# A forward table held twice and the work of the first steps laid out anew in a fused FFT filter and feed-forward kernel

## The chip, the cores and the metric

The kernel runs on one core of a Trainium2 chip. The metric is the device time of one execution in microseconds. TensorE (PE) multiplies matrices and writes PSUM, VectorE (DVE) and ScalarE (ACT) read PSUM and SBUF, GpSimd (POOL) and SyncE (SP) here only issue DMA transfers, each in its own queue, in order. POOL's transfers convert fp32 to fp16 on the way where the tiles differ in type; it has up to eight in flight, since it waits for the ninth last transfer's semaphore to be used again.

## The reference

`x` is [8, 3008, 256]: eight batches of 3008 tokens with 256 channels. Each channel is filtered in the frequency domain along the tokens, and the result goes through a feed-forward layer with a slope for negative values.

```python
X = np.fft.rfft(x, axis=1)
Y = X * (filt_r + 1j * filt_i)[None]
y = np.fft.irfft(Y, n=3008, axis=1).reshape(24064, 256)
h = y @ w_in                                       # 256 -> 2048
g = np.maximum(h, 0) + alpha * np.minimum(h, 0)
out = g @ w_out                                    # 2048 -> 256
```

## The kernel before, in words

**The transform.** 3008 is 94 x 32. A batch goes through four stages, each a set of small matmuls and evictions. Piece a (`piece_a`, eight per batch, L155) is the transform of length 94; ACT evicts it into `asb`, `save_a` stores `asb` to DRAM and `turn_a` reads it back as `at` in another layout. Piece b (`piece_b`, six per batch, L179) is the transform of length 32 with its twiddles from the table `twf_s`, and DVE multiplies the result by the filter and by a copy of the filter with rows exchanged (`filt_s`, `filts_s`, L186 and L187). The two products are added across partitions by transfers in POOL's queue: added into `uu` by the transfer itself for batch one (L191), and for later batches brought into `sw` (L193) and added by DVE (`piece_s`). Piece c (`piece_c`, six per batch, L210) is the inverse of length 32 with `twi_s`; ACT evicts it to `v`, and `turn_c` stores it to DRAM and, after the last piece, reads it back as `zt`. Pairs d (`pair_d`, eight per batch, L232) are the inverse of length 94 and evict to `yT`, the transposed input of the feed-forward layer. Group g of four (752 tokens each) of a batch is its pairs 2g and 2g+1.

**Batch zero** is done by a class of its own, `First`, without DRAM: it turns tiles by matmuls with a unit matrix (`turn_at` L289, `half_t` and `piece_t` L340), uses a second table `twx_s` so that no exchange of rows is needed, and goes in twelve passes `kp` (L408 to L419): `piece_b(kp + 2)` (L299), `piece_c(kp)` (L323), evictions to `v`. In its piece b every matmul uses a tile of 64 rows and 32 columns of PE, sixteen per pass, since each half of the table's 64 columns has to be written to two places of PSUM. DVE's multiplication per pass is L303. Its first pass takes the filter from an fp32 tile `fst`, loaded by SP; the others from `filt_s`, loaded by POOL as three parts (`load_filt`, rows 1 to 3, 4 to 7, 8 to 11). `fst` has the tag "asb": it shares its one buffer with batch one's `asb`. After the loop POOL copies `fst` into `filt_s` (L420) and builds `filts_s` from it (L423, L425); DVE later negates parts of `filts_s` (`neg`, L545). `warm` (L382) multiplies a unit matrix into a bank that is then overwritten: filling work for PE. `half_t` and `half_d` of group zero end this part.

**The feed-forward layer** runs in 48 blocks of 512 or 384 tokens, twelve for two batches, 16 steps each: 768 steps. In step j a block's `up` does two matmuls of 512 columns (L466); after every second one ACT evicts both (L475) into a ring of nine slots `gtb`, and DVE does the slope with `alm_s` (L478, two per eviction; L480 once per four steps). `down` (L497, four matmuls per step for 512 tokens) is that of the block before. ACT evicts the output to `osb` (L502) and SP stores it (L448).

**The order** is written out by hand (`manual_schedule`): engines execute in program order, and semaphores follow from the tiles. A dictionary `plan` says which pieces go into which step (L506 to L562). They run before the step's `up`; in a step that has a piece a or c (`front`) the step's `down` goes first. The first block has no block before it, so steps 0 to 15 have no `down`. Before the change batch zero's groups one to three lie in steps 0 to 33 (L536 to L542): group one as halves, groups two and three as whole pieces. Batch one has its pieces a at even steps 12 to 26, `turn_a` at 28, pieces b at 36 to 66 (every six steps), pieces c at 48 to 78, pairs d from 91. The loads of x for batch two are put at steps 17 to 29; they are POOL instructions and wait in its queue, not for the step itself but for a free buffer (four of them, `p_x`) and for the instructions ahead. `banks(False)` is one PSUM tile `psF` of two banks with one buffer; `banks(True)` is `hps`, two buffers, which `up`, pieces a and c share; `bank("o")` is `op`, two buffers.

**Tables and slopes.** SP loads the tables of batch zero in two parts, columns 0 to 8 first (L364, L367) and 8 to 24 after the sixth piece a (L390 to L395). A tiny `memset` by DVE on the part to be loaded (L391) holds that load back until then. The slopes come from `al16` by a transpose on PE (L397) and two DVE instructions (L398, L399) after the sixth piece a.

Of the kernel before, what the change touches and what calls it, by code (L numbers as in the profile page):

```python
# [16 lines left out]
D = 256  # L17
# [33 lines left out]
def kernel(  # L51
# [211 lines left out]
    class First(Fft):  # L263
        def __init__(self):
            super().__init__(0)
            self.at = p_fft.tile([128, NK, D], FP16, name="at")
            self.v = p_fft.tile([128, NK, D], FP16, name="v")
            self.zt = p_fft.tile([96, N2, D], FP16, name="zt")
            self.fst = p_fft.tile([128, 1, 2, D], FP32, name="fst", tag="asb")
            self.am = gtb[:, 0:6].rearrange("p a b c -> p (a b c)")  # L270
            self.vm = self.v.rearrange("p k d -> p (k d)")

# [19 lines left out]
        def piece_b(self, kp):  # L292
            hp = psH.tile([128, 2, 512], FP32, name="hps").rearrange("p r (i d) -> p r i d", i=2)
            for i in range(2):
                for par in range(2):
                    r = slice(64 * par, 64 * par + 64)
                    for o in (0, 32, 64, 96):
                        k = 2 * kp + o // 64
                        nc.tensor.matmul(hp[o : o + 32, par, i], twf_s[r, k, 32 * i : 32 * i + 32],  # L299
                                         self.at[r, k], start=True, stop=True, tile_position=(64 * par, o))  # L300
            uu = p_uw.tile([128, 2, 2, D], FP16, name="uu", bufs=3)
            fl = self.fst if kp < 1 else filt_s
            nc.vector.tensor_mul(uu, hp, fl[:, kp].unsqueeze(2).to_broadcast([128, 2, 2, D]))  # L303
            self.uw[kp] = uu

        def piece_c(self, kp):
            if kp % 2 == 0:
                self.ops = [psO.tile([128, 2, D], FP32, name="op") for _ in range(2)]
            if kp == 11:
                pf = banks(False)  # L310
                warm(5, pf[:, 0])
                self.ops = [pf[:, e].rearrange("p (k d) -> p k d", k=2) for e in range(2)]
            kb = 0 if kp == 11 else kp % 2
            u = self.uw.pop(kp)
# [1 line left out]
            for par in range(2):  # L316
                for f in range(2):
                    for i, t in enumerate((tw, tx)):
                        for e in range(2):
                            r = slice(64 * e, 64 * e + 64)  # L320
                            o = self.ops[e][:, kb].rearrange("p (g w) -> p g w", g=16)
                            o = o[:, 8 * f : 8 * f + 8, 8 * par : 8 * par + 8]
                            nc.tensor.matmul(o.rearrange("p g (c e) -> p g c e", c=2),  # L323
                                             u[r, par, i, 128 * f : 128 * f + 128], t[r, 2 * kp + par],
                                             start=(i == 0), stop=(i == 1))

        def keep_c(self, kp, evicts, n=2):
            vm = self.vm.rearrange("p (g q k e) -> p g q k e", q=4, k=NK, e=4)
# [31 lines left out]

    xc = {(0, c): load_x(0, c) for c in range(4)}
    f0 = First()
    load_filt(nc.sync, f0.fst, 0, 1)
    tables(nc.sync, ("twf",), 0, 8)  # L364
    nc.sync.dma_start(out=al16, in_=moe_alpha.rearrange("(j p) -> j p", p=128))
    nc.sync.dma_start(out=id32, in_=id32_d.ap())
    tables(nc.sync, ("twi", "twx"), 0, 8)  # L367
    load_filt(nc.gpsimd, filt_s, 1, 4)
    load_filt(nc.gpsimd, filt_s, 4, 8)
    load_filt(nc.gpsimd, filt_s, 8, 12)  # L370
# [15 lines left out]
    for i in range(8):  # L386
        f0.piece_a(i, both[i % 2], i % 3 < 2)
        if i % 2 == 1:
            warm((4, 4, 8, 3)[i // 2], bank("o"))
        if i == 5:  # L390
            nc.vector.memset(twf_s[:, 8:24, 0:1], 0.0)  # L391
            tables(nc.sync, ("twf", "twi", "twx"), 8, 24)
            nc.sync.dma_start(out=wi3_s, in_=consts["wi3"].ap())
            nc.sync.dma_start(out=wf1_s, in_=consts["wf1"].ap())
            nc.sync.dma_start(out=sgn_s, in_=sgn_d.ap())  # L395
            alp = psO.tile([128, 2, D], FP32, name="op")
            nc.tensor.transpose(alp[:, 0, 0:16], al16, id32)  # L397
            nc.vector.tensor_copy(al_s, alp[:, 0, 0:16])  # L398
            nc.vector.tensor_scalar(alm_s, al_s, 1.0, -1.0, OP.mult, OP.add)  # L399
    f0.turn_at(0, 1, on_act)  # L400
    f0.turn_at(1, 1, on_dve, True)
    warm(2, bank("o"))
# [25 lines left out]
        f0.half_t(i, evict, kind)  # L428
    for i, evict, kind, fill in ((0, on_act, "h", 1), (2, on_dve, "o", 0), (1, on_act, "o", 1), (3, on_dve, "f", 0)):
        f0.half_d(i, evict, kind, fill)  # L430


    sizes = [512] * 5 + [384] + [512] * 6
# [99 lines left out]
        for i in range(8):  # L533
            put(d_at[i], f.pair_d, i, on_act)

    for i in range(4):  # L536
        put(i, f0.half_t, 4 + i, both[i % 2], "o")
        put(6 + i, f0.half_d, 4 + (0, 2, 1, 3)[i], both[i % 2], "o")
    for g, ts, ds, evict in ((2, (13, 15), (21, 23), on_dve), (3, (25, 27), (31, 33), on_act)):
        for i in range(2):  # L540
            put(ts[i], f0.piece_t, 2 * g + i, evict)
            put(ds[i], f0.pair_d, 2 * g + i, evict)  # L542

    def neg(ha, hb):
        nc.vector.tensor_scalar(filts_s[:, ha:hb], filts_s[:, ha:hb], sgn_s[:, 0:1], None, OP.mult)  # L545

    for i in range(4):
        put(16 + 2 * i, neg, 3 * i, 3 * i + 3)

    def d_steps(p):  # L550
        return [p + t for t in (91, 93, 104, 108, 116, 120, 140, 152)]

    plan_fft(1, range(12, 28, 2), 28, 4, (17, 21, 25, 29), range(36, 72, 6), 0, range(48, 84, 6),
             (91, 93, 98, 101, 110, 120, 142, 154))
    plan_fft(2, (50, 56, 62, 68, 74, 80, 82, 84), 90, 4, (57, 69, 81, 85), (104, 114, 126, 136, 148, 158), 7,
             (114, 126, 136, 148, 158, 170), d_steps(96))
    for b in range(3, NB):
        p = 96 * (b - 1)
        a_at = (10, 16, 22, 28, 34, 36, 44, 48) if b == 3 else (6, 10, 18, 22, 30, 34, 42, 46)
# [53 lines left out]
```

## Time and profile before

| | |
|---|---|
| time, median of three | 786.81 us (785.9 to 788.47) |
| profiled execution: time | 788.27 us |
| profiled execution: span in the trace | 786.5 us |
| PE busy | 770.0 us (98%), 6450 matmuls |
| DVE busy | 596.2 us (76%) |
| ACT busy | 583.0 us (74%) |
| POOL busy (issuing transfers) | 142.3 us (18%) |
| first up-projection (L466) | 41.28 us |
| first eviction of batch one's piece a | 50.58 us |
| up-projection of step 16 | 56.37 us |
| up-projection of step 36 | 81.60 us |

The span runs from the first to the last record; the time has some 1.8 us around it. All places are microseconds from the span's start. A busy PE is not PE at its peak, because overlapping matmuls are all counted as busy; so stages are compared by the length of their steps, which the L466 records give, and by what PE waits for between them. "Idle before, releaser" in a timeline is the time that an engine stood still ahead of a group and what ended it; "issue" means that the profile shows nothing that it waited for. "DMA issues to landing" is measured from the start of the issuing instruction.

### The profile page before, as it was taken

To read this page: it belongs to the slowest core of one execution; us is meant where nothing else is said; L and a number is where in the kernel's file an instruction comes from. 1 tells how busy PE (TensorE), PEld (TensorE's weight loads), DVE (VectorE), ACT (ScalarE), POOL (GpSimd) and SP (SyncE) were. 2 spreads that over 40 slices of the span, in tenths; PEclk is the share of its full clock that TensorE was granted. 3 is DMA by queue.
4 is the path that set the end of the run, shared out by engine and by line. 5 is a ranking of instruction groups with operands and counts; after the bars stand their busy time and mean duration, and the time that the engine had idled before them with its cause. 6 is when DMAs were issued, how large, how long until landed. Compare 5 with 4: busy or idle time off the path is not lost.

```text
span 786.5 us, 16280 instructions
## 1 busy us (share of the span) xinstructions
PE 770.0 (98%) x6450; PEld 512.1 (65%) x6450; DVE 596.2 (76%) x1117; ACT 583.0 (74%) x671; POOL 142.3 (18%) x271
## 2 busy tenths in 40 slices
PE   7889999999999999999999999999999999999997
PEld 3556566666666666766666666766666666766665
DVE  3686895788868887788867888688877888766663
ACT  3578688788778887798777887788876777677663
POOL 6512362132202220022201222010100111000000
PEclk9999999999999999999999999999999999999999
DMA  9978688756664657555593655834474233511112
GB/s 197 166 162 194 148 162 171 229 132 158 140 167 109 145 137 146 136 119 130 126 200 88 143 125 134 191 82 108 115 148 129 56 86 93 143 42 28 41 41 55
DMA packets 95084, 100.66 MB, mean 128 GB/s; under 512 B 11280, under 2 KB 82464, under 8 KB 94816
## 3 DMA queue, kind: packets, MB, share of 16 engines
q1 hardware_dynamic: 80368, 70.25, 34.2%
q0 software_dynamic: 14640, 29.38, 21.6%
q8 instruction: 50, 0.82, 0.4%
q14 instruction: 26, 0.21, 0.1%
HBM read 55.28 MB, written 46.66 MB: 130 GB/s over the span
## 4 chain that ended last, share of the span: by engine, by line
PE 88%; DMA 8%; POOL 1%; ACT 1%; DVE 1%; issue 1%; SPq 0%; ACTq 0%; POOLq 0%
PE op L497 40%; PE hps L466 40%; DMA xs<-in_x_dram 3%; PE hps L155 3%; PE psF L232 2%; DMA a_dram<-asb 2%; PE psF L179 2%; PE hps L210 1%; DMA filts_s<-filt_s 1%; DMA filt_s<-fst 1%; DMA filt_s<-in_filt_r_dram 1%; POOL filt_s L122 1%; DMA at<-a_dram 1%; POOL xs L112 0%; ACT gtb L475 0%
## 5 line engine op out<-in xcount | busy, mean ns | idle before, releaser
L475 ACT ACTIVATE gtb<-hps 128x1024 f16<-128x1024 f32 (+1 forms) x384 | 385.8, 1005 | 136.9 <-PE hps L466 132.7
L466 PE MATMUL hps<-yT,win_s 128*128 128x512 f16 (+1 forms) x1536 | 435.1, 375 | 1.8 <-ACT gtb L475 1.5
L497 PE MATMUL op<-wout_s,gtb 128*128 128x256 f16 x3008 | 435.8, 273 | 0.1
L497 PEld LDWEIGHTS <-gtb 128*128 128x128 f16 x3008 | 294.0, 98 | 168.3 <-issue 0.4
L478 DVE TENSOR_SCALAR m<-gtb,alm_s 128x512 f16<-128x512 f16 (+1 forms) x768 | 232.9, 346 | 148.0 <-ACT gtb L475 147.1
L480 DVE TENSOR_TENSOR gtb<-gtb,m 128x2048 f16<-128x2048 f16 (+1 forms) x192 | 231.0, 1203 | 10.1
L466 PEld LDWEIGHTS <-win_s 128*128 128x128 f16 x1536 | 142.6, 98 | 59.7 <-issue 15.3
L193 POOL DMA_DIRECT2D sw<-ww x144 | 70.8, 500 | 383.8 <-DVE ww L186 380.9
L255 ACT ACTIVATE asb<-hps 96x1024 f16<-96x1024 f32 x56 | 57.1, 1020 | 11.7 <-PE hps L155 11.2
L502 ACT ACTIVATE osb<-op 128x512 f32<-128x512 f32 (+1 forms) x97 | 56.2, 579 | 5.3 <-issue 2.8
L255 ACT ACTIVATE v<-hps 128x1024 f16<-128x1024 f32 x42 | 43.0, 1024 | 14.3 <-PE hps L210 14.3
L255 ACT ACTIVATE yT<-psF 128x752 f16<-128x752 f32 x58 | 46.2, 797 | 8.5 <-PE psF L232 8.5
L112 POOL DMA_DIRECT2D xs<-in_x_dram x64 | 35.5, 597 | 92.0 <-PE hps L155 77.0
L186 DVE TENSOR_TENSOR ww<-psF,filts_s 128x1024 f16<-128x1024 f32 x42 | 51.1, 1216 | 0.0
L187 DVE TENSOR_TENSOR uu<-psF,filt_s 128x1024 f16<-128x1024 f32 x42 | 51.0, 1213 | 0.0
L155 PE MATMUL hps<-xs,wf_s 94*96 94x512 f16 x112 | 33.4, 379 | 0.2 <-ACT gtb L475 0.2
L232 PEld LDWEIGHTS <-zt 96*128 96x128 f16 x512 | 28.8, 98 | 5.0 <-issue 2.1
L232 PE MATMUL psF<-wi_s,zt 96*128 96x94 f16 x484 | 30.3, 206 | 0.5 <-DVE yT L258 0.5
L198 DVE TENSOR_TENSOR uu<-uu,sw 128x1024 f16<-128x1024 f16 x36 | 24.6, 684 | 1.2 <-DMA sw<-ww 1.2
L191 POOL DMA_DIRECT2D uu<-ww x24 | 19.2, 1219 | 28.0 <-DVE uu L187 23.7
L179 PE MATMUL psF<-at,twf_s 64*64 64x256 f16 x336 | 17.9, 281 | 1.8 <-DMA at<-a_dram 1.8
L210 PE MATMUL hps<-uu,twi_s 64*64 64x256 f16 x336 | 16.5, 271 | 0.0
(64 smaller groups left out, 175.0 us busy)
## 6 DMA issues: line engine op xcount, KB each, us to landing
out_dram<-osb SPq DMA_DIRECT2D x160, 128.0 KB
a_dram<-asb SPq DMA_DIRECT2D x28, 384.0 KB
v_dram<-v SPq DMA_DIRECT2D x84, 128.0 KB
zt<-v_dram SPq DMA_DIRECT2D x28, 384.0 KB
sw<-ww POOLq DMA_DIRECT2D x144, 64.0 KB, 2.5
at<-a_dram SPq DMA_DIRECT2D x20, 384.0 KB
xs<-in_x_dram POOLq DMA_DIRECT2D x32, 192.0 KB, 4.4
xs<-in_x_dram POOLq DMA_DIRECT2D x32, 184.0 KB, 5.8
```

Of the source, the lines that this page charges most:

```text
L155: nc.tensor.matmul(ps[0:96, u], wf1_s, xs[:, o : o + 512], start=True, stop=True)
L186: nc.vector.tensor_mul(ww, px, fs)
L187: nc.vector.tensor_mul(uu, px, f)
L193: nc.gpsimd.dma_start(out=sw[o : o + 32], in_=ww[i : i + 32])
L232: nc.tensor.matmul(ps[:, m], self.zt[:, 8 * g + 4 * mh + m, dh * 128 : dh * 128 + 128], wi3_s, start=True, stop=True)
L255: nc.scalar.activation(o, i, AF.Copy)
L466: nc.tensor.matmul(self.hps[:, j % 2, 0:tn], win_s[:, kt, j * 128 : (j + 1) * 128], yT[:, kt, self.t0 : self.t0 + tn], start=(kt == 0), st ...
L475: nc.scalar.activation(g[:, 2 * i : 2 * i + 2], self.hps[:, :, 0:tn], AF.Copy)
L478: nc.vector.tensor_scalar(m[:, 2 * i + h], g[:, 2 * i + h], 0.0, a, OP.min, OP.mult)
L480: nc.vector.tensor_add(g, g, m)
L497: nc.tensor.matmul(self.op[:, si - s0], self.gts[k][:, 128 * si : 128 * si + 128], wout_s[:, k], start=(si == s0 and k == 0), stop=(si == ...
L502: nc.scalar.activation(osb[:, 0:m], self.op[:, 0:m], AF.Copy)
```

## The change

In `First`, the forward table is kept a second time as `twd`, in a part of the ring `gtb` that is not in use yet, with each half of 32 columns written twice side by side, so that piece b needs eight matmuls with tiles of 64 rows and 64 columns instead of sixteen. `twice` makes it in three copies: columns 0 to 8 on ACT after the sixth piece a, 8 to 16 on ACT and 16 to 24 on DVE after the eighth. SP's loads are put in another order: table `twf` first, then `fst`, held back by a `memset` until the second piece a is evicted, and after the sixth piece a `twf`, `twi`, `twx`, the slopes and the small tables. The transpose of the slopes moves behind group zero. The last pass fills with two matmuls instead of five. Groups one to three are whole pieces, later than before for group two, and `neg` moves to steps 26 to 35. For batch one the pieces b and c move by two steps and some pairs d by one; the loads of x for batch two are put at 34, 42, 54 and 66 (between the pieces b), and some pieces of batch two move by two to four steps. Later batches keep their plan.

```diff
+            self.twd = gtb[:, 6:9].rearrange("p a b c -> p (a b c)").rearrange("p (k m) -> p k m", m=128)
...
-                    for o in (0, 32, 64, 96):
-                        k = 2 * kp + o // 64
-                        nc.tensor.matmul(hp[o : o + 32, par, i], twf_s[r, k, 32 * i : 32 * i + 32],
-                                         self.at[r, k], start=True, stop=True, tile_position=(64 * par, o))
+                    for e in range(2):
+                        nc.tensor.matmul(hp[64 * e : 64 * e + 64, par, i],
+                                         self.twd[r, 2 * kp + e, 64 * i : 64 * i + 64], self.at[r, 2 * kp + e],
+                                         start=True, stop=True)
...
-                warm(5, pf[:, 0])
+                warm(2, pf[:, 0])
...
+        def twice(self, ka, kb, copy):
+            o = self.twd[:, ka:kb].rearrange("p k (i c m) -> p (k i) c m", i=2, c=2)
+            w = twf_s[:, ka:kb].rearrange("p k (i m) -> p (k i) m", i=2)
+            copy(o, w.unsqueeze(2).to_broadcast([128, 2 * (kb - ka), 2, 32]))
...
-    load_filt(nc.sync, f0.fst, 0, 1)
     tables(nc.sync, ("twf",), 0, 8)
-    nc.sync.dma_start(out=al16, in_=moe_alpha.rearrange("(j p) -> j p", p=128))
-    nc.sync.dma_start(out=id32, in_=id32_d.ap())
-    tables(nc.sync, ("twi", "twx"), 0, 8)
...
+        if i == 1:
+            nc.vector.memset(f0.fst[:, 0, :, 0:1], 0.0)
+            load_filt(nc.sync, f0.fst, 0, 1)
         if i == 5:
+            f0.twice(0, 8, on_act)
             nc.vector.memset(twf_s[:, 8:24, 0:1], 0.0)
-            tables(nc.sync, ("twf", "twi", "twx"), 8, 24)
+            tables(nc.sync, ("twf",), 8, 24)
+            tables(nc.sync, ("twi", "twx"), 0, 8)
+            tables(nc.sync, ("twi", "twx"), 8, 24)
             nc.sync.dma_start(out=wi3_s, in_=consts["wi3"].ap())
+            nc.sync.dma_start(out=al16, in_=moe_alpha.rearrange("(j p) -> j p", p=128))
+            nc.sync.dma_start(out=id32, in_=id32_d.ap())
...
-            alp = psO.tile([128, 2, D], FP32, name="op")
-            nc.tensor.transpose(alp[:, 0, 0:16], al16, id32)
-            nc.vector.tensor_copy(al_s, alp[:, 0, 0:16])
-            nc.vector.tensor_scalar(alm_s, al_s, 1.0, -1.0, OP.mult, OP.add)
+    f0.twice(8, 16, on_act)
+    f0.twice(16, 24, on_dve)
     f0.turn_at(0, 1, on_act)
...
         f0.half_d(i, evict, kind, fill)
+    alp = bank("o")
+    nc.tensor.transpose(alp[:, 0:16], al16, id32)
+    nc.vector.tensor_copy(al_s, alp[:, 0:16])
+    nc.vector.tensor_scalar(alm_s, al_s, 1.0, -1.0, OP.mult, OP.add)
...
-    for i in range(4):
-        put(i, f0.half_t, 4 + i, both[i % 2], "o")
-        put(6 + i, f0.half_d, 4 + (0, 2, 1, 3)[i], both[i % 2], "o")
-    for g, ts, ds, evict in ((2, (13, 15), (21, 23), on_dve), (3, (25, 27), (31, 33), on_act)):
+    for g, ts, ds, te, de in ((1, (0, 3), (6, 12), on_act, both[::-1]), (2, (19, 23), (25, 28), on_dve, (on_dve, on_dve)),
+                              (3, (31, 33), (35, 37), on_act, (on_act, on_act))):
         for i in range(2):
-            put(ts[i], f0.piece_t, 2 * g + i, evict)
-            put(ds[i], f0.pair_d, 2 * g + i, evict)
+            put(ts[i], f0.piece_t, 2 * g + i, te)
+            put(ds[i], f0.pair_d, 2 * g + i, de[i])
...
-        put(16 + 2 * i, neg, 3 * i, 3 * i + 3)
+        put(26 + 3 * i, neg, 3 * i, 3 * i + 3)
...
-    plan_fft(1, range(12, 28, 2), 28, 4, (17, 21, 25, 29), range(36, 72, 6), 0, range(48, 84, 6),
-             (91, 93, 98, 101, 110, 120, 142, 154))
-    plan_fft(2, (50, 56, 62, 68, 74, 80, 82, 84), 90, 4, (57, 69, 81, 85), (104, 114, 126, 136, 148, 158), 7,
-             (114, 126, 136, 148, 158, 170), d_steps(96))
+    plan_fft(1, range(12, 28, 2), 28, 4, (34, 42, 54, 66), range(38, 74, 6), 0, range(50, 86, 6),
+             (91, 93, 97, 100, 111, 121, 142, 154))
+    plan_fft(2, (48, 52, 58, 64, 70, 76, 82, 84), 90, 4, (57, 69, 81, 89),
+             (106, 116, 126, 136, 148, 158), 7, (116, 126, 136, 148, 158, 172), d_steps(96))
```

The arguments of `plan_fft` are: batch, steps of the pieces a, step of `turn_a`, into how many parts it is cut, steps of the loads of x for the next batch, steps of the pieces b, steps from b to `piece_s` (0: the transfer adds), steps of the pieces c, steps of the pairs d.

## The prediction

> **What bounds the kernel now.** First the page's busy time and chain, then a table of busy time by stretches of ten microseconds, to see where TensorE (PE) is not the limit.
>
> ```profile
> span 786.5 us, 16280 instructions
> PE 88%; DMA 8%; POOL 1%; ACT 1%; DVE 1%; issue 1%; SPq 0%; ACTq 0%; POOLq 0%
> ```
> ```profile
> 40.00:50.00 10.00, 8.92 (x72) 5.39 (x69) 7.98 (x17) 7.97 (x12) 1.70 (x4) 1.00 0.61 110
> 50.00:60.00 10.00, 8.76 (x58) 5.57 (x57) 7.90 (x15) 7.74 (x9) 2.41 (x5) 1.00 0.91 224
> 80.00:90.00 10.00, 9.04 (x71) 5.74 (x72) 8.67 (x14) 4.68 (x6) 3.19 (x4) 1.00 0.79 186
> 160.00:170.00 10.00, 10.00 (x74) 6.73 (x73) 8.05 (x16) 8.06 (x10) 2.99 (x6) 1.00 0.47 98
> ```
> The second column is PE's busy time. From 90 us on PE is full; a step there is two L466 and four L497 matmuls, 0.87 us. The change leaves that stage's work as it is, so it can win only before about 160 us. Next the chain of what ended last, in order of time (start, us, what), cut to its long transfers.
>
> ```profile
> 27.26 15.45 DMA xs<-in_x_dram
> ...
> 43.03 6.11 DMA filt_s<-fst
> ...
> 70.60 7.00 DMA a_dram<-asb
> ...
> 79.05 2.17 DMA at<-a_dram
> ...
> 81.26 0.41 PE psF L179 x6
> ```
> Two transfers matter (a landing, here and below, is the last increment of the transfer's semaphore in the trace). `filt_s<-fst` reads the tile `fst`, which shares its space (tag "asb") with batch one's `asb`: ScalarE's first `asb` eviction cannot start before it lands, at 49.14. And `at<-a_dram` holds the first L179 group of batch one. Last, the timelines of PE, VectorE (DVE) and ScalarE (ACT) where the first loop ends.
>
> ```profile
> 30.41 0.30 PE L299 MATMUL hps<-at,twf_s 64*32 64x256 f16 x7
> 31.98 0.38 PE L299 MATMUL hps<-at,twf_s 64*32 64x256 f16 x9 [1.27 <-issue]
> ...
> 34.20 2.32 PE L382 MATMUL psF<-id 128*128 128x512 f16 x5
> ```
> ```profile
> 27.77 3.48 DVE L303 TENSOR_TENSOR uu<-hps,filt_s 128x1024 f16<-128x1024 f32 x3 [0.22 <-DMA filt_s<-in_filt_i_dram]
> 32.40 1.23 DVE L303 TENSOR_TENSOR uu<-hps,filt_s 128x1024 f16<-128x1024 f32 x1 [1.14 <-PE hps L299]
> ```
> ```profile
> 50.58 1.02 ACT L255 ACTIVATE asb<-hps 96x1024 f16<-96x1024 f32 x1
> ```
> ```profile
> 30.71:34.12 3.41, 1.69 (x43) 0.95 (x42) 1.77 (x2) 1.08 (x2) 0.53 (x2) 1.00 1.28 192
> 34.12:37.53 3.41, 3.41 (x33) 1.32 (x26) 0.01 (x1) 1.04 (x3) 0.52 (x1) 0.50 1.44 207
> ```
> The loop's twelve multiplications (1.15 us each) bind it; the ninth waits for the filter, at 27.64. PE's gap of 1.27 us falls inside a group, after an instruction transfer of 16,384 bytes that ran from 29.72 to 30.61; the stretch with PE at 1.69 of 3.41 us is followed by one at a granted clock of 0.50, in which five filling matmuls took 2.32 us.
>
> **The change part by part.**
>
> *Table held twice.* L299 loses 96 matmuls with their weight loads. That saves nothing by itself: PE waits for DVE in this loop. It adds two copies of 128x1024 on ACT and one on DVE. No row has an fp16 copy of this shape from SBUF; DVE's 128x512 row (346 ns, twice: 0.69 us) is below it, ACT's eviction of 128x1024 (1.02 us) beside it; I take 1.02 on ACT, and up to 1.2 on DVE. The first ACT copy fits into ACT's idle 2.70 us before 15.06. The second waits for table columns 8 to 24, which landed at 16.46, 3.5 us after their issue. Bounds for that landing: as quick as the first transfer of all (0.74 to 2.35) it is 13.7; as slow as the first table piece (5.28 to 13.62) it is 21.3. I take 15.7, the old delay with an issue 0.75 earlier. Then the copy ends at 16.7, where ACT started its first `at` eviction at 16.93.
>
> *Slopes loaded last.* The transpose at 14.38 waited for its tables; PE had been free since 13.58 and x had landed at 13.08. That is 0.8 to 1.1 us early, which the copies then use up. The loop starts between 17.2 and 18.1 instead of 18.06, and the ninth multiplication still waits for the filter: no gain up to 27.7. The moved transpose and its two DVE rows (0.17 each) sit before the first slope multiplication, where DVE idles 0.86.
>
> *End of the loop.* With 16 fewer PE instructions per pass, the place where the gap fell (about PE's 950th instruction) moves behind the loop, into the inverse transforms. The twelfth multiplication then runs from 31.25 to 32.4, and the last L323 group, behind two filling matmuls instead of five, ends at about 33.05 instead of 37.0: 3.9 us.
>
> *What of that survives.* Up-projections then start near 38.2 (41.28; the larger first piece of group one costs 0.4 and a wait of 0.6 for its bank). ACT owes twelve steps six evictions of 1.0, two of 1.02 and one of 0.80, so it reaches the first `asb` eviction near 46.8 and waits for 49.14. Against 50.58 that is 1.44 us; the other 2.4 are a new wait. Behind it, steps 12 to 15 no longer hold the two pieces of group two (eight L340 matmuls, 0.65 us each, and DVE evictions of 1.21): their period falls from 2.8 us per two steps to ACT's 2.05. Step 16's up-projection starts at 53.1 instead of 56.37: **3.3 us**.
>
> *Steps 16 to 38.* Before, 56.37 to 83.34, of which 0.68 and 0.44 were waits for banks and 1.85 the wait for `at` in step 35: 24.0 us of work. The two pieces of group two now lie here (1.3), and I allow 0.6 of new bank waits: 25.9. `at` is no longer late: the last save is issued near 66.1, and even with the old 7.0 us the first reads are out at 75, before step 38 near 78. So **1.1 more**, 4.4 in all.
>
> *x of batch two later.* GpSimd's queue runs ahead of the steps until an instruction waits; the first pair goes out near 60 as before, and the other three now wait behind the `uu<-ww` additions of batch one, which wait for DVE. They are out at steps 39, 51 and 63, needed at 58, 70 and 82: over ten microseconds, where x took 7 to 8. What they may delay are the additions behind them. These land 1.3 to 3.5 us before their L210 group needs them; the set issued 5 us behind x (110.43) landed 1 us later than the undisturbed ones. I take **-0.3** (bounds 0 and the fourth rival).
>
> *Later steps.* L210 of the last piece moves from step 78 to 80, its consumers stay at 91. The work between was 11.2 us and is now 8.9. The path was: eviction 1.1, stores issued 126.03 to 127.88 and landed 131.6, reads issued 131.71, first matmul 136.32. The x load that ran beside the stores (127.5) is now issued after step 76, ahead of them; stores could land 2.1 us after issue as at step 57's, then the wait is 0.4 to 0.8; with nothing faster it is 2.5, before it was 0.3. I take **-0.4**. Batch two's first piece, two steps later, loses its 0.49 us wait for `at`: **+0.5**. Three pieces at steps 48, 50, 52 crowd ACT: **-0.2**. The negations of the filter (four times 0.6 us on DVE) move from 16-22 to 26-35, where DVE has as much room.
>
> *Clock.* The new 2.4 to 2.9 us without PE work before 50.15 leaves a 3.41 us stretch with PE under 1.7 us unless a boundary halves it; 1.69 was enough for 0.50 above. Half a clock for 3.41 us takes at most 1.7 us, less what ACT would have held PE anyway: **-1.0** (0 to -1.5). The Trainium skill (TensorE: Matmul & The Clock Gate, "HAM oscillation") asks only that PE not idle longer than about 3.4 us; by that rule this gap costs nothing, and the result is the second rival. The trace speaks against it, since its longest gap ahead of the half clock was 1.27 us.
>
> **Sum.** 3.3 + 1.1 - 0.3 - 0.4 + 0.5 - 0.2 - 1.0 = 3.0 us less than the profiled execution's 788.27, or 785.3. That execution lay 1.46 above the median of 786.81, perhaps through the very gap at 30.41, which only costs the 1.44 above; taken from the median instead, the sum gives 783.8. I predict **784.0**. A difference under 0.3% (2.4 us) can hardly be told from none.
>
> **Rivals.**
> 1. *The early gain is swallowed*: the table lands at 21.3 instead of 15.7. The loop then starts 5 us later, its end gains nothing, and ACT reaches `asb` 2 us after the landing. 785.5 to 787.5. For it: DMA is above 90% busy in those slices; against: the pieces that were ahead of this table are now behind it.
> 2. *No half clock, no wait at step 91*: 1.0 and 0.4 come back, and a bank wait or two: 781 to 782.5.
> 3. *Copies shorter or moved work does nothing*: the pieces of group two cost at 19 and 23 what they cost at 13 and 15, since each was a bank wait: 1.5 us less gain, 785.5.
> 4. *Slower: additions behind x.* Place: steps 50 to 80. An x load took up to 8.3 us from issue to landing (105.35 to 113.65). If the additions of pieces one, three and five land that much later, less 3.5, 1.6 and 1.3 of room, PE waits 4.8 + 6.7 + 7.0 = 18.5 us: 802. It turns the result from 4.4 us later per set on (6.9 us in all). For it: DMA share 0.95 between 100 and 110. The Trainium skill (Trainium Kernel Development and Optimization, "Key Constraints") has all queues share the same DMA engines, which the 1 us of the 110.43 set agrees with.
>
> **Chances.** Forecast (782 to 785.5) 0.48, split 0.36 beyond 0.3% and 0.12 within; rival 1, 0.15, and rival 3, 0.09, both within; rival 2, 0.16, faster; rival 4, 0.12. So faster 0.52, same 0.36, slower 0.12. The range for 8 in 10 leaves out rival 4 and the far end of rival 2: 780.5 to 788.0.
>
> **What would show it.** Right: no gap inside an L299 group, no clock of 0.50 near 34; ACT idle before its first `asb` eviction, released by `filt_s<-fst` near 49; L466 of step 16 near 53; no DMA wait before the first L179 of batch one. Wrong: the second 128x1024 copy on ACT ending after 18; PE waiting before L210 for `uu<-ww`; a wait of over 1 us for `zt` at step 91; or `filt_s<-fst` landing elsewhere, since the sum hangs on it.

## The result, and the profile after

The changed kernel takes 791.03 us, the median of 22 runs (787.2 to 795.01); the kernel before, on the same chip, 787.65 us (22 runs, 785.55 to 788.95). The ratio is 1.0044, with an interval of 1.003 to 1.0058: the change makes the kernel **slower by 0.44%**, where 784.0 us was forecast. The new time lies outside the range of 780.5 to 788.0.

The profiled execution doesn't show that by its length. It took 788.28 us, the same as the profiled one before (788.27), and its span is the same too. From the page of the changed kernel, the span, the chain of what ended last, and the one group whose wait is new:

```profile
span 786.5 us, 16089 instructions
...
PE 93%; DMA 3%; ACT 2%; DVE 1%; issue 1%; SPq 0%; POOL 0%; ACTq 0%; POOLq 0%
...
L232 PE MATMUL psF<-wi_s,zt 96*128 96x94 f16 x500 | 31.3, 206 | 2.3 <-DMA zt<-v_dram 2.1
```

The same group on the page of the kernel before:

```profile
L232 PE MATMUL psF<-wi_s,zt 96*128 96x94 f16 x484 | 30.3, 206 | 0.5 <-DVE yT L258 0.5
```

DMA on the chain went from 8% to 3%, so transfers did leave the path; but L232, the inverse transform of the later batches, now waits 2.1 us for `zt`. The table of busy time by stretches (the second column is PE's):

```profile
80.00:90.00 10.00, 9.99 (x86) 6.40 (x85) 9.01 (x16) 6.50 (x8) 4.41 (x6) 1.00 0.53 108
130.00:140.00 10.00, 7.85 (x72) 5.84 (x71) 4.40 (x11) 5.75 (x9) 0.99 (x2) 1.00 0.88 220
```

Between 80 and 90, PE went from 9.04 to 9.99 us: the wait for `at` is gone, as forecast. Between 130 and 140 PE stands still for 2.15 us. The start of the first loop, in the timelines of ScalarE (ACT), PE and VectorE (DVE):

```profile
17.59 1.06 ACT L255 ACTIVATE gtb<-twf_s 128x1024 f16<-128x1024 f16 x1 [3.20 <-DMA twf_s<-c_twf]
```
```profile
15.46 0.59 PE L384 MATMUL op<-id 128*128 128x512 f16 x2
19.18 0.41 PE L299 MATMUL hps<-at,gtb 64*64 64x256 f16 x8 [3.12 <-ACT at L255]
19.53 1.03 PE L290 MATMUL psF<-id,gtb 128*128 128x128 f16 x8
20.49 0.64 PE L299 MATMUL hps<-at,gtb 64*64 64x256 f16 x8
```
```profile
19.64 1.23 DVE L304 TENSOR_TENSOR uu<-hps,fst 128x1024 f16<-128x1024 f32 x1 [1.01 <-PE hps L299]
21.19 1.23 DVE L304 TENSOR_TENSOR uu<-hps,filt_s 128x1024 f16<-128x1024 f32 x1 [0.32 <-DMA filt_s<-in_filt_i_dram]
23.35 9.14 DVE L304 TENSOR_TENSOR uu<-hps,filt_s 128x1024 f16<-128x1024 f32 x8 [0.94 <-PE hps L299]
```

Columns 8 to 24 of the table landed at 17.50. The copy on ACT waited for them, the first `at` eviction stood behind the copy, and PE had no work for over 3 us ahead of its first L299 group. Then the same eight matmuls took 0.64 us at 20.49 and 0.41 at 19.18, and eight transposes 1.03 where those at 24.25 took 0.62: the clock had been halved. (The DVE line at 21.19 names a filter transfer as what ended its wait; those rows had landed at 15.78, and what it waited for is PE's slow group, 20.49 to 21.13.) The table by stretches of 3.41 us, set on the bounds of the clock's record (the last three numbers are the granted clock, the DMA share and GB/s):

```profile
16.10:19.51 3.41, 0.33 (x8) 0.14 (x7) 1.03 (x2) 1.54 (x2) 2.47 (x5) 1.00 1.09 227
19.51:22.92 3.41, 3.41 (x34) 2.07 (x34) 2.45 (x2) 1.03 (x1) 0.77 (x2) 0.50 1.08 207
```

PE worked 0.33 us of one stretch and got half a clock in the next. The forecast had its one half-clock stretch near 50, behind a wait of ACT for `filt_s<-fst`. That wait isn't there: in the changed kernel the transfer had landed by 47.19, and ACT came to its first `asb` eviction only at 51.54, with no idle time before it.

```profile
51.54 1.02 ACT L255 ACTIVATE asb<-hps 96x1024 f16<-96x1024 f32 x1
```

The profiled execution was a lucky one: its mean granted clock is 0.998, while the 22 runs have 0.990 to 0.998, 0.9946 on average. A straight line through the 22 pairs of time and clock rises by 7.2 us for each 0.01 of clock lost and passes 787.1 us at full clock. The clock lost, (1 - 0.9946) x 786.5 = 4.2 us, is 2.5 stretches of 3.41 us at half clock; the kernel before, at 0.998 in the experiments below, loses 1.6 us. So up to 2.6 of the 3.4 us between the medians go with the clock. It may be all of them: the same line through the 89 runs of the kernel before that stand beside the experiments is much flatter, 2.7 us for each 0.01, and also passes 787.1 us at full clock.

### The profile page after: what moved, and what is told of

It is laid out like the page before. It is cut to its first block, busy times and chain, and to the rows that moved or that the text cites. A ratio compares the mean times of both kernels' runs of the same rounds, so it can differ in the third digit from the quotient of the medians.

```text
span 786.5 us, 16089 instructions
## 1 busy us (share of the span) xinstructions
PE 768.0 (98%) x6351; PEld 511.5 (65%) x6351; DVE 595.7 (76%) x1116; ACT 585.9 (74%) x672; POOL 142.8 (18%) x271
## 4 chain that ended last, share of the span: by engine, by line
PE 93%; DMA 3%; ACT 2%; DVE 1%; issue 1%; SPq 0%; POOL 0%; ACTq 0%; POOLq 0%
PE hps L478 41%; PE op L509 41%; PE hps L155 3%; PE psF L232 3%; PE psF L179 2%; PE hps L210 1%; ACT gtb L487 1%; ACT v L255 1%; PE psF L346 1%; DMA xs<-in_x_dram 1%; DMA fst<-in_filt_r_dram 1%; PE op L324 1%; DMA twf_s<-c_twf 1%; DMA v_dram<-v 1%; DMA zt<-v_dram 0%
## 5 line engine op out<-in xcount | busy, mean ns | idle before, releaser
L478 PE MATMUL hps<-yT,win_s 128*128 128x512 f16 (+1 forms) x1536 | 434.0, 375 | 1.5 <-ACT gtb L487 1.4
L478 PEld LDWEIGHTS <-win_s 128*128 128x128 f16 x1536 | 142.8, 98 | 61.0 <-issue 14.5
L112 POOL DMA_DIRECT2D xs<-in_x_dram x64 | 39.2, 707 | 80.8 <-PE hps L155 69.0
L232 PE MATMUL psF<-wi_s,zt 96*128 96x94 f16 x500 | 31.3, 206 | 2.3 <-DMA zt<-v_dram 2.1
L232 PEld LDWEIGHTS <-zt 96*128 96x128 f16 x512 | 28.5, 98 | 5.0 <-DMA zt<-v_dram 2.4
L210 PE MATMUL hps<-uu,twi_s 64*64 64x256 f16 x336 | 16.5, 271 | 0.0
```

What stands on the lines that cost most here:

```text
L232: nc.tensor.matmul(ps[:, m], self.zt[:, 8 * g + 4 * mh + m, dh * 128 : dh * 128 + 128], wi3_s, start=True, stop=True)
L478: nc.tensor.matmul(self.hps[:, j % 2, 0:tn], win_s[:, kt, j * 128 : (j + 1) * 128], yT[:, kt, self.t0 : self.t0 + tn], start=(kt == 0), st ...
```

## The experiments

**Theory**: the planned gain is there, and two waits take it back: PE's gap ahead of the first loop, through the clock behind it, and the wait for `zt` at step 91. **Rivals**: the doubled table and its wider matmuls are slower by themselves; the new plan of the later batches is; the later loads of x are.

One table for all, since they are read together. "Clock lost" is (1 - mean granted clock) x 786.5 us, an estimate of what the half-clock stretches cost, and too high where PE would have waited for others anyway; the last column is the median less that. The experiments ran on three chips, each with the kernel before beside them, and the ratio is to that one. Its medians there were 787.86 (e1 to e4), 787.32 (e5 to e8) and 787.77 us (e9 to e12), its "rest" 786.4, 785.7 and 786.0. So half a microsecond between kernels of different chips tells nothing.

| kernel | median us | ratio to before, interval | clock lost | rest |
|---|---|---|---|---|
| before | 787.65 | 1 | 1.6 | 786.1 |
| after | 791.03 | 1.0044 (1.003 to 1.0058) | 4.2 | 786.8 |
| e1 after, pairs d later | 788.83 | 1.0004 (0.9986 to 1.0023) | 3.3 | 785.5 |
| e2 after, table once | 790.37 | 1.0031 (1.0017 to 1.0045) | 4.0 | 786.4 |
| e3 before, with the head of after | 789.79 | 1.0033 (1.0018 to 1.0048) | 3.7 | 786.1 |
| e4 after, with before's batches | 794.08 | 1.0088 (1.0063 to 1.0113) | 5.5 | 788.6 |
| e5 before, with the plan of after | 789.2 | 1.0032 (1.0011 to 1.0053) | 2.9 | 786.3 |
| e6 e5, pairs d later | 786.64 | 0.9997 (0.9976 to 1.0018) | 1.7 | 784.9 |
| e7 after, first gap filled | 787.74 | 1.0005 (0.9993 to 1.0016) | 1.4 | 786.3 |
| e8 after, filling ahead of the `zt` wait | 791.23 | 1.005 (1.0032 to 1.0068) | 3.9 | 787.4 |
| e9 e7, pairs d later | 784.13 | 0.9962 (0.995 to 0.9973) | 0.1 | 784.0 |
| e10 e7, x of batch two early again | 788.17 | 1.001 (0.9998 to 1.0023) | 1.6 | 786.5 |
| e11 e3, first gap filled | 787.86 | 1.0003 (0.9992 to 1.0014) | 0.6 | 787.3 |
| e12 after, whole table loaded first | 788.13 | 1.001 (0.9998 to 1.0023) | 2.6 | 785.6 |

**e1: the pairs d of batch one one or two steps later.**

```diff
-             (91, 93, 97, 100, 111, 121, 142, 154))
+             (93, 94, 99, 102, 111, 121, 142, 154))
```

> The changed kernel with four pairs d of batch one a little later (91, 93, 97, 100 become 93, 94, 99, 102); nothing else. Theory A: the wait for zt ahead of step 91 (2.3 us in the trace of the changed kernel, and half-clock stretches that follow such a gap) is what makes the change slower. Two more steps of 0.76 us in front of it then take 1.5 us of the wait away, and some of the half clocks: about 788 to 789.5 against 791.0. Theory B: the gap of 3.3 us at 15.7, where PE waits for the table copies, does it: no change from 791. Theory C: the x loads of batch two beside the additions: no change from 791.

Measured: 788.83 us, 2.2 less than the change. PE's wait for `zt` is down to 1.12. The first gap is as in the change, and this profiled execution shows what it can bring; its stretches:

```profile
15.00:18.41 3.41, 1.04 (x10) 0.68 (x11) 0.33 (x1) 0.34 (x1) 2.68 (x6) 1.00 1.04 218
18.41:21.82 3.41, 2.16 (x25) 1.19 (x25) 1.92 (x3) 1.71 (x3) 1.80 (x4) 0.50 1.12 243
21.82:25.24 3.42, 3.42 (x46) 1.86 (x42) 2.18 (x2) 1.54 (x2) 2.00 (x5) 0.50 0.92 129
```

One gap, two stretches of half clock in a row: it began before 18.41 and went on into the first of them. A third followed at 35.48. What follows: the wait for `zt` is a real part of the loss. Whether it is the whole, this run can't tell, since the interval of its ratio has 1 inside.

**e2: the table held once**, sixteen matmuls of 32 columns again, all else as changed.

```diff
-                    for e in range(2):
-                        nc.tensor.matmul(hp[64 * e : 64 * e + 64, par, i],
-                                         self.twd[r, 2 * kp + e, 64 * i : 64 * i + 64], self.at[r, 2 * kp + e],
-                                         start=True, stop=True)
+                    for o in (0, 32, 64, 96):
+                        k = 2 * kp + o // 64
+                        nc.tensor.matmul(hp[o : o + 32, par, i], twf_s[r, k, 32 * i : 32 * i + 32],
+                                         self.at[r, k], start=True, stop=True, tile_position=(64 * par, o))
...
-            f0.twice(0, 8, on_act)
...
-    f0.twice(8, 16, on_act)
-    f0.twice(16, 24, on_dve)
```

> The changed kernel with the forward table not held twice: no copies, piece b of batch zero with sixteen matmuls of 32 columns as before; loads and all plans as in the changed kernel. Theory A: the zt wait stays, so 790 to 791. Theory B: the gap at 15.7 and the half clock behind it go, the loop starts 2 us earlier, and the time falls to 787.5 to 789. Theory C: 791.

Measured: 790.37 us. Without the copies the first multiplication starts at 16.46 instead of 19.64, yet the fifth then waits for the filter, in DVE's timeline:

```profile
24.05 3.49 DVE L304 TENSOR_TENSOR uu<-hps,filt_s 128x1024 f16<-128x1024 f32 x3 [2.62 <-DMA filt_s<-in_filt_r_dram]
```

The gap has only moved, to 22.8 (2.51 us), and half a clock follows at 26.47. So the doubled table isn't what costs: what is saved ahead of the loop is lost inside it, because rows 4 to 7 of the filter land at 23.92 (22.30 before the change). The wait for `zt` is in this kernel too, 3.53 us in this execution, with two stretches of half clock at 135.69.

**e3: the kernel before with the new head alone** (the doubled table and the order of the loads), plans as before.

```diff
-    for g, ts, ds, te, de in ((1, (0, 3), (6, 12), on_act, both[::-1]), (2, (19, 23), (25, 28), on_dve, (on_dve, on_dve)),
+    for i in range(4):
+        put(i, f0.half_t, 4 + i, both[i % 2], "o")
+        put(6 + i, f0.half_d, 4 + (0, 2, 1, 3)[i], both[i % 2], "o")
+    for g, ts, ds, evict in ((2, (13, 15), (21, 23), on_dve), (3, (25, 27), (31, 33), on_act)):
...
-        put(26 + 3 * i, neg, 3 * i, 3 * i + 3)
+        put(16 + 2 * i, neg, 3 * i, 3 * i + 3)
...
+    plan_fft(1, range(12, 28, 2), 28, 4, (17, 21, 25, 29), range(36, 72, 6), 0, range(48, 84, 6),
+             (91, 93, 98, 101, 110, 120, 142, 154))
```

> The kernel before with only the head of the change (table twice, order of the loads, slopes later, two filling matmuls instead of five); groups, negations and the plans of batches one and two as before. Theory A: as before or faster, 785.5 to 788. Theory B: slower than before, 789 to 791. Theory C: as before, 787.5.

Measured: 789.79 us, 1.0033 of before: the head alone loses. In this profiled execution the first gap of 2.66 us did not cost half a clock, since a bound at 17.28 cut it in two; a shorter one at 61.9 did:

```profile
63.79 0.49 PE L232 MATMUL psF<-wi_s,zt 96*128 96x94 f16 x8 [1.87 <-DVE yT L258]
```
```profile
61.66:65.07 3.41, 1.54 (x17) 0.99 (x15) 3.41 (x7) 1.20 (x2) 1.28 (x3) 1.00 0.98 207
65.07:68.48 3.41, 3.41 (x18) 2.25 (x17) 2.42 (x4) 2.22 (x3) 0.00 (x0) 0.50 0.94 173
```

**e4: the change with before's plans of batches one and two.**

```diff
-    plan_fft(1, range(12, 28, 2), 28, 4, (34, 42, 54, 66), range(38, 74, 6), 0, range(50, 86, 6),
-             (91, 93, 97, 100, 111, 121, 142, 154))
+    plan_fft(1, range(12, 28, 2), 28, 4, (17, 21, 25, 29), range(36, 72, 6), 0, range(48, 84, 6),
+             (91, 93, 98, 101, 110, 120, 142, 154))
...
```

> The changed kernel with the plans of batches one and two (steps of the pieces, loads of x) as before; head and whole pieces of batch zero as in the change. Theory A: the zt wait goes back to 0.3 us, the wait for at in step 35 returns (1.85 us): 788 to 789.5. Theory B: 791. Theory C: below 790, with the additions landing as before.

Measured: 794.08 us, worse than every other kernel and well beside its expectation. The timeline of PE says why:

```profile
84.08 0.51 PE L232 MATMUL psF<-wi_s,zt 96*128 96x94 f16 x8 [3.29 <-DVE uu L187]
```

Batch one's first piece b, at step 36, lies between batch zero's late pairs d at 35 and 37; the second of these waits for its bank until DVE is done with the piece, and half a clock follows at 84.91. The mixture has a wait that neither kernel has, so its time tells nothing on the theories. Its trace tells one thing: with the pieces c back at their old steps, PE doesn't wait for `zt` ahead of step 91. That the new plan puts the pieces b two steps later is needed by its own later pairs d.

**e5: the kernel before with the new plan alone; e6: the same with the pairs d later.** The head is before's: sixteen matmuls per pass, slopes early, five fillings in the last pass.

```diff
-             (91, 93, 97, 100, 111, 121, 142, 154))
+             (94, 95, 99, 102, 111, 121, 142, 154))
```

> The kernel before with only the plan of the change (groups one to three as whole pieces, negations later, batches one and two and the loads of x as in the change); head as before, with the table once and the old order of loads. Theory A (the wait for zt ahead of step 91 is the main loss, the head the smaller one): gains in steps 12 to 38 of about 2.7 us and the zt wait of about 2.2 nearly cancel, 787 to 788.5. Theory B (the head is the whole loss): clearly faster than before, 784 to 786.

> The same, and the first four pairs d of batch one at 94, 95, 99, 102, so that zt has 2.3 us more. Theory A: the gains stay and the wait goes, 784.5 to 786, faster than before. Theory B: as the kernel with the plan alone, 784 to 786, no difference between the two.

Measured: 789.2 and 786.64 us, both a little above what either theory gave. Two or three steps of delay are worth 2.6 us, 1.4 of them beside the clock; e5 waits 2.23 us for `zt`, e6 not at all. Whether the plan without its wait is faster than before is not shown: on the same chip its median is 0.7 us lower (786.64 against 787.32), but the interval of the ratio, 0.9976 to 1.0018, has 1 well inside. It still has before's gap inside an L299 group and the half clock behind it, here in e6:

```profile
32.25 0.58 PE L299 MATMUL hps<-at,twf_s 64*32 64x256 f16 x9 [1.54 <-issue]
```
```profile
28.85:32.26 3.41, 1.71 (x46) 0.73 (x45) 1.74 (x2) 0.64 (x2) 0.51 (x1) 1.00 1.19 200
32.26:35.67 3.41, 3.37 (x45) 1.50 (x45) 1.22 (x1) 1.62 (x4) 0.54 (x1) 0.50 1.45 198
```

**e7: the first gap filled.** Sixteen filling matmuls instead of two ahead of the first piece b; PE works on through the gap, and nothing else changes.

```diff
-    warm(2, bank("o"))
+    warm(16, bank("o"))
```

> The changed kernel with sixteen filling matmuls instead of two ahead of the first piece b of batch zero, which is about the 3.3 us in which PE waits for the table there. No work is added to any path, if they are done when the table is. Half clock follows from PE standing still: the granted clock rises from 0.9946 in the mean to 0.996 or more and the time falls by about 1 us, to 790. Rival (the half clocks have nothing to do with this gap): 791 and the same mean clock.

Measured: 787.74 us, 3.3 less than the change, where 1 was expected; 2.9 of it is clock. PE and DVE in the timelines of e7:

```profile
15.38 3.62 PE L384 MATMUL op<-id 128*128 128x512 f16 x16
18.93 0.41 PE L299 MATMUL hps<-at,gtb 64*64 64x256 f16 x8
```
```profile
22.01 11.42 DVE L304 TENSOR_TENSOR uu<-hps,filt_s 128x1024 f16<-128x1024 f32 x10 [0.26 <-PE hps L299]
```

The first multiplication starts at 19.40, no earlier than in the change within a quarter of a microsecond, but ten of them now follow one another without a gap, and the last ends at 33.4 instead of 35.97. So the gap cost little by its length, since the loop waits for the same table either way. Of the 2.5 us at the loop's end, 1.1 are the pauses right behind the half clock (between the first and the third multiplication); another 1.2 lie around a second gap of PE, at 31.0, which comes up again below. This kernel still has the wait for `zt`, and in its profiled execution the wait fell whole into one stretch:

```profile
131.79:135.20 3.41, 1.02 (x14) 0.66 (x13) 0.65 (x3) 0.12 (x2) 0.00 (x0) 1.00 0.93 263
135.21:138.62 3.41, 3.41 (x22) 2.31 (x20) 1.51 (x3) 1.52 (x3) 0.00 (x0) 0.50 0.95 275
```

**e8: ten filling matmuls ahead of batch one's first pair d**, to fill the wait for `zt` in the same way.

```diff
+            if self.b == 1 and i == 0:
+                warm(10, ps[:, 0])
```

> The changed kernel with ten filling matmuls (2.1 us) in PE ahead of the first pair d of batch one, where it waits 2.3 us for zt. The wait itself stays. If the wait costs through the half clock behind it as well, the mean clock rises by 0.001 to 0.002 and the time falls by about 1 us, to 790; if only through its length, 791 and the same clock.

Measured: 791.23 us, as the change. PE's timeline:

```profile
132.87 2.32 PE L386 MATMUL psF<-id 128*128 128x512 f16 x10
137.79 0.51 PE L232 MATMUL psF<-wi_s,zt 96*128 96x94 f16 x8 [2.60 <-DMA zt<-v_dram]
```

The fillings were done at 135.2 and PE then waited 2.60 us: here the last store took 5.10 us to land and the read of `zt` 3.82 instead of 3.13, and PE got `zt` 0.9 later than in the change. The gap was behind the filling instead of filled, and half a clock followed at 139.09. So the run doesn't tell what the wait costs by length and what by clock; it shows that filling wins nothing where the wait outlasts it.

**e9: both cures**, the fillings of e7 and the later pairs d of e6.

```diff
-    warm(2, bank("o"))
+    warm(16, bank("o"))
...
-             (91, 93, 97, 100, 111, 121, 142, 154))
+             (94, 95, 99, 102, 111, 121, 142, 154))
```

> The changed kernel with both cures that worked alone: sixteen filling matmuls ahead of the first piece b of batch zero, and the first four pairs d of batch one at 94, 95, 99, 102. If the half clocks after the first gap (3.3 us) and the wait for zt (2.2 to 2.6 us) are two separate losses, they add up: 791.0 - 3.3 - 2.2 = 785.5 or a little less, faster than before by about 2 us. If they are one loss seen twice (the same half clocks): 787.5.

Measured: 784.13 us, 0.9962 of before (0.995 to 0.9973): **faster than both kernels**, at a granted clock of 0.9999. The two cures together take 6.9 us off the change, 3.3 and then 3.6 (2.3 beside the clock). The lines of ACT, DVE and PE in e9 that answer to those above:

```profile
49.23 1.02 ACT L255 ACTIVATE asb<-hps 96x1024 f16<-96x1024 f32 x1
```
```profile
22.25 11.41 DVE L304 TENSOR_TENSOR uu<-hps,filt_s 128x1024 f16<-128x1024 f32 x10 [0.26 <-PE hps L299]
```
```profile
134.55 0.50 PE L232 MATMUL psF<-wi_s,zt 96*128 96x94 f16 x8
```

The first pair d of batch one waits for nothing. Nor does the first `asb` eviction: `filt_s<-fst` had landed at 48.78, and ACT came straight from other work.

**e10: x of batch two at its old steps**, on top of e7.

```diff
-    plan_fft(1, range(12, 28, 2), 28, 4, (34, 42, 54, 66), range(38, 74, 6), 0, range(50, 86, 6),
+    plan_fft(1, range(12, 28, 2), 28, 4, (17, 21, 25, 29), range(38, 74, 6), 0, range(50, 86, 6),
```

> The changed kernel with the sixteen filling matmuls, and the loads of x for batch two put at steps 17 to 29 as before; pairs d at 91. If the later loads of x crowd the stores and reads of v ahead of step 91, the zt wait falls from 2.5 to about 1.5 us and the wait for at in step 35 to 38 comes back in part (up to 1.5 us): about equal, 787 to 788.5. If the wait comes only from the two steps by which the pieces c are later, it stays at 2.3 to 2.6 and the time goes up to 788 to 789.5.

Measured: 788.17 us against e7's 787.74, and the intervals overlap; the time lies in both of the expected ranges. The wait for `zt` is 1.94 us (2.39 in e7, one execution each), between the two expectations. So the moved loads make at most half a microsecond of the wait, and no cost of theirs shows.

**e11: the filling with the head alone**, on top of e3.

```diff
-    warm(2, bank("o"))
+    warm(16, bank("o"))
```

> The kernel before with the head of the change alone (789.8) and sixteen filling matmuls ahead of the first piece b of batch zero. If the head's loss is the half clocks behind the gap: 787 to 788, as before. If the head loses through its longer wait and its order of loads: 789.5 to 790.

Measured: 787.86 us, 1.9 less than e3, all of it in the clock column and more (3.7 to 0.6). A gap is left, as the table landed at 18.31 here:

```profile
20.00 0.27 PE L299 MATMUL hps<-at,gtb 64*64 64x256 f16 x1 [1.32 <-ACT at L255]
```

With the filling the head alone is level with before (1.0003), although before loses about 1 us more to the clock: by itself it brings nothing here. Together with the new plan it does better, 786.64 (e6) against 784.13 (e9), 0.9 us of it beside the clock; the two ran on different chips.

**e12: the whole table loaded first**, ahead of x, and no filling added: the gap goes because its cause goes.

```diff
-    tables(nc.sync, ("twf",), 0, 8)
+    tables(nc.sync, ("twf",), 0, 24)
...
-            nc.vector.memset(twf_s[:, 8:24, 0:1], 0.0)
-            tables(nc.sync, ("twf",), 8, 24)
```

> The changed kernel, the whole forward table loaded by SP ahead of fst in one transfer instead of columns 8 to 24 after the sixth piece a; no filling matmuls added, pairs d at 91. The gap of 3.3 us then has no reason: the copies run when ACT and DVE are free, the loop starts near 17.5 instead of 19.6, no half clock, and the time is that of the kernel with sixteen filling matmuls or below: 787 to 788. If the half clocks come from something else in the new head: 790 to 791.

Measured: 788.13 us, 2.9 less than the change. The table landed at 6.45, and the loop starts at 18.44. This kernel keeps the wait for `zt`, with half a clock behind it in the profile (134.55). So filling as such isn't what helped in e7: without the gap, by either way, 2.9 to 3.3 us come back. In e7 2.9 of the 3.3 stand in the clock column, in e12 1.7 of the 2.9; e12 also starts its loop 1.2 us earlier.

## Why the prediction was wrong

By its own steps, from the starts of the steps (L466 before, L478 after). "With both cures" is e9, whose trace has no half clock ahead of its end. Gains against the profiled execution before, in us:

| step of the sum | forecast | changed kernel's trace | with both cures |
|---|---|---|---|
| to step 16 (56.37 before) | 3.3 | 0.7 (55.72) | 3.0 (53.41) |
| steps 16 to 38 (83.34) | 1.1 | 0.8 (81.86) | 0.8 (79.55) |
| steps 38 to 90 (135.37): additions behind x | -0.3 | 0.1 (133.81) | 0.1 (131.50) |
| step 90 to 91 (136.66): `zt` | -0.4 | -2.1 (137.20) | 0.5 (132.26) |
| step 91 to the end (span 786.5) | 0.3 | 0.5 (786.5) | -0.1 (782.2) |
| clock | -1.0 | in the first line | none |
| sum | 3.0 | 0.0 | 4.3 |

(In e9, 0.3 us of the gain from step 90 to 91 has only moved into the next row, with the pair d that went from step 91 to 94.)

*Right*: the later layout. Steps 12 to 16 are lighter as worked out: from the first `asb` eviction to step 16 it was 5.79 us and is 4.18 (51.54 to 55.72), a gain of 1.6 of the 1.9 forecast. The wait for `at` at step 38 is gone. The additions behind x delayed nothing: there is no DMA wait ahead of an L210 group, so the fourth rival, the slower one, was not what made it slower.

*Right by luck*: the place of the first `asb` eviction, forecast at 49.14 and at 49.23 in e9. The forecast had the loop's last multiplication end at 32.4, the up-projections start near 38.2, and ACT stand at `asb` from 46.8 on, waiting for `filt_s<-fst`. In e9, without any half clock, the last multiplication ends at 33.66, no earlier than before (33.63), and the up-projections start at 40.28. ACT so comes to `asb` 2.4 us later than forecast, by chance just behind the landing. "End of the loop" thus failed in the cured kernel too: the loop starts at 19.64 there instead of 17.2 to 18.1, which uses up what was to be gained inside it. The inverse transforms behind it end earlier than before (35.16 against 37.06) because two filling matmuls at full clock (0.60 us) stand where five at half clock did (2.32). The wait of ACT for `filt_s<-fst`, from which the forecast took its -1.0 of clock, stands in one of the fourteen traces, that of e3, with 0.27 us:

```profile
49.00 1.02 ACT L255 ACTIVATE asb<-hps 96x1024 f16<-96x1024 f32 x1 [0.27 <-DMA filt_s<-fst]
```

*The step that failed most: "Clock"*, with "Table held twice" ahead of it. The forecast took one stretch at half clock, -1.0, behind a gap near 47 to 50, and expected the stretch at 34 to go. The place was wrong, and the size was. The table landed at 17.50, inside the bounds of 13.7 to 21.3 and 1.8 later than the value taken; the copy took 1.06 us (1.02 taken) and ended at 18.65, past the 18 that was named as the sign of a wrong forecast. The first rival had this late table, but priced it as delay alone, at 785.5 to 787.5. What it missed is that PE has nothing to do meanwhile: 3.12 us without a matmul, and half a clock in the loop, whose later pauses then bring further stretches (e1: two in a row and one at 35.48). Filling the gap gives 3.3 us (e7), removing its cause 2.9 (e12).

Whether a gap costs clock depends on where the bounds of the 3.41 us stretches fall. In the traces of the two kernels and the twelve experiments, from 10 to 200 us, all 14 stretches in which PE was busy for 1.71 us or less (half a stretch) were followed by one at 0.50; of those that began at full clock and held 1.8 to 2.2 us of work, two were and ten were not; above 2.2 none was. The bounds lie elsewhere in each run. The wait for `zt` in the change shows a lucky cut, two stretches of which neither is half empty:

```profile
132.15:135.56 3.41, 2.58 (x21) 1.77 (x19) 1.97 (x5) 2.01 (x3) 0.00 (x0) 1.00 0.76 177
135.56:138.97 3.41, 2.10 (x26) 1.76 (x27) 0.03 (x1) 1.50 (x2) 0.00 (x0) 1.00 0.87 223
```

With half a stretch as the limit and PE busy all around, a gap of 2.3 us stays under it in (2 x 1.71 - 2.3) / 3.41 = 33% of the placings, one of 3.1 us in 9%. That is an estimate from the counts above, not measured; a share that varies from run to run would give a spread like that of the changed kernel's clock (0.990 to 0.998), but no run tests it. The Trainium skill (TensorE: Matmul & The Clock Gate, "Part 1: The HAM clock gate") has a free-running window of 3413 ns, with which these stretches agree. Its rule in "HAM oscillation", no idle gaps of over about 3.4 us, by which the second rival's 781 to 782.5 came about, doesn't hold here: gaps of 3.12 us in the change, 2.39 in e7 and 1.87 in e3 were followed by half a clock.

*The second: "Later steps", -0.4 for `zt`.* It lists the wait as 0.4 to 0.8 if the stores land 2.1 us after issue, and 2.5 "with nothing faster". The second came: PE waits 2.13 us, more than the 1 us that was named as a sign of a wrong forecast. The chain of the change from that place (start, us, what):

```profile
125.76 1.03 ACT v L255
...
129.54 3.96 DMA v_dram<-v
...
133.69 3.13 DMA zt<-v_dram
...
136.87 0.51 PE psF L232 x8
```

The last store took 3.96 us from issue to landing, as slow as before (127.41 to 131.56, 4.15), and the four issues on SP took 2.95 us instead of 1.85. The loads of x that were to be out of the way were replaced by the next: two were issued at 129.95. Two stores of the output, issued at 125.90 and 126.49, stood right ahead in SP's queue, where before had none; what they cost was not tried. The price over both wait and clock is 2.2 to 3.6 us (after to e1, e5 to e6, e7 to e9; the first and the last pair are not of one chip). The -0.4 was taken from the better of two branches of which the worse had the trace of before behind it.

*Smaller misses.* "The place where the gap fell moves behind the loop": a gap is still in the loop of the change, now inside an L324 group:

```profile
32.04 0.20 PE L324 MATMUL op<-twi_s,uu 64*128 64x64 f16 x1 [1.03 <-issue]
```

It fell at about PE's 705th instruction in the trace, before's at the 960th, so the place is not a matter of their number. Both stand right behind an instruction transfer of 16,384 bytes (29.59 to 30.55 in the change, 29.72 to 30.61 before); with the first gap filled or its cause removed (e7, e9, e12) there is no gap over 0.5 us in the loop. Why is open. DVE's copy took 0.43 us where up to 1.2 was allowed. The base, a median of three runs at 786.81, was 0.8 below that of the 22 runs, and the sum took its gains from there. By its own terms the fourth rival's 6.9 us are 6.8.

With both losses gone, 3.3 + 1.1 - 0.3 + 0.5 - 0.2 = 4.4 was forecast, and e9's span is 4.3 shorter than that of before's profiled execution; by the medians on one chip it is 3.6. That the totals agree is in part luck: the rows are off by 0.3 to 0.5 us each, both ways, and the first holds the chance named above. By the "rest" column the change has 0.7 us over before beside the clock (786.8 against 786.1), by the two lines at full clock nothing (787.1 and 787.1); which is so stays open.

## What to carry to other kernels

When a producer is moved by two steps, look at each consumer's due time again: the last piece c went from step 78 to 80 and the first pair d stayed at 91, and giving the pairs d two or three steps more won 2.2 to 3.6 us. Ahead of a wait that can't be shortened, keep PE busy up to its end. In kernels like this one, count any stretch in which PE would stand still for half of 3.4 us as a likely stretch at half clock, with its price in what runs behind it and not in the gap. One profiled execution can be a lucky one: compare the granted clock of all runs before a trace is taken for the kernel.

## What the runs showed of the hardware that was not expected

- The spread of the changed kernel's times goes largely with the clock: over its 22 runs, 7.2 us for each 0.01 of mean granted clock. It need not be so: over 89 runs of the kernel before it was 2.7 us, and e9, at 0.9999, ran from 783.96 to 786.95 us.
- The copy of 128x1024 fp16 values from SBUF to SBUF took 0.43 us on DVE and 1.06 on ACT, no less than ACT's eviction of the same shape in fp32 from PSUM (1.02). By these rows it would be shorter on DVE; that was not run.
- The order of SP's loads moved transfers of another queue: the filter's rows 4 to 7, issued by POOL, landed at 24.04 in the change and at 22.30 before, while its rows 1 to 3 came 2.3 us earlier (15.78 against 18.04).
